# One-hot loads on another queue, an identity made on VectorE, two clears on GpSimd, and the mask tile's row copy issued earlier, in a fused block-sparse attention and low-rank mixer kernel

## The chip, the cores and the metric

The kernel runs on one core of a Trainium2 chip. The core has five engines that run side by side: TensorE (PE in the profile) for matrix products, with its weight load shown apart as PEld; VectorE (DVE); ScalarE (ACT); GpSimd (POOL); and SyncE (SP), which here only issues DMAs. The ending "q" (SPq, ACTq, POOLq) marks the sequencer of an engine, which issues DMAs and waits on semaphores. The metric is the device time of one execution in microseconds, lower is better.

## What is computed

Sparse attention over blocks of 32 tokens, then a mixer with a low-rank product along the sequence and a two-layer network. The reference, cut to what matters:

```python
B, H, S, D = 4, 8, 768, 64                 # q, k, v: float32
mask = window | first and last block row and column | 3 sampled blocks per row
scores = where(mask, q @ k.T / sqrt(D), -1e9)
attn   = softmax(scores) @ v
x = attn.transpose(0, 2, 1, 3).reshape(B, S, H * D)
u = x + (x.T @ U @ V).T                    # U: 768x32, V: 32x768
out = u + relu(u @ w_ch1) @ w_ch2          # w_ch1: 512x2048, w_ch2: 2048x512
```

## The kernel before

**Tiling.** The 4 x 8 heads are taken as 16 pairs of heads of one batch. Tokens lie as 128 partitions by T = 6. For each pair, q and k are loaded (`qld`, `kld`, L153, or L182 for the first pair), cast to fp16 (`stqld`, `stkld`), turned so that the head dimension lies on partitions, and then, for each block of 128 keys, TensorE makes scores transposed (keys on partitions, all 768 queries along the row), ScalarE takes exp into `est` (L996 for one block, L1014 for two), and TensorE multiplies `est` with `vt` (L421), whose 65th column of ones gives the sum. VectorE divides (L551, L558).

**Two ways to mask.** For the first four pairs (batch 0) the mask is added inside the score product: the operands `qres` and `kres` (parts of the tile `res`) hold 64 rows of q or k and 24 more rows. In `qres` the 24 rows are a one-hot code of the query's block (`one_hot_const`, 24 x 768); in `kres` they are the mask bias of each key column. There are two such sets, `qres[0]`/`kres[0]` for pairs 0 and 2 and `qres[1]`/`kres[1]` for pairs 1 and 3. Within a set the two heads of the pair use the rows 64 to 87 and 0 to 23 (`mrows`), the unused rows being zero. For the later pairs a 0/1 tile `mask` is multiplied after exp (L1052). `mask` is made in twelve pieces by products of the tile `kmask` (24 bias rows, the rest zero) with `qres[0]` (`mask_part`, L946, evaluated by VectorE at L952).

**The start.** The body of the kernel up to line 349 is written out by hand: each engine runs its instructions in exactly the order in which they are written (`manual_schedule`). It loads q and k of the first pair, one head at a time (`first_load`), the constants `small` (block mask, indices and an fp16 identity) and the sampled blocks `sb` (L245, L246, ScalarE's queue). TensorE runs idle products (`keep_warm`, L272) until the data is there. The first head is turned straight from fp32 with an fp32 identity `id32` (L226); the result is copied into `qres[0]` and `kres[0]` by ScalarE and VectorE (`first_row`, L297). Meanwhile VectorE makes the bias from `sb` (L311, L315, L318); the product of bias and one-hot rows (`mask_half`, L279) gives the 24 mask rows, which `mask_row` (L287) copies into `kres[0]`. The second head of the first pair is cast by GpSimd (L213), turned from fp16 (`last_turn`, L359) and copied (L366).

**After the start** a long string `PLAN` gives the order of everything else: each word is one step (S and B scores, e their exp, A value products, R the turning of the next pair's q or k, K one `mask_part`, and so on). The engines follow it in order.

**Queues.** SP issues nearly all loads, one after the other: an issue that has to wait holds up all that is written behind it. The order on SP at the start is: q and k of head 0; the two one-hot loads of `qres[0]` (L187); q and k of head 1; v of pair 0; q, k and v of pair 1; U (L200); then `second_set` (L192 to L196): one-hot rows and a copy of the mask rows for each head of set 1, and last the copy of the mask rows to `kmask`; then V (L206) and the loads of pair 2. The loads on SP and ScalarE report on eight completion semaphores, used in turn in program order, so that the ninth load waits until the first one has landed, and so on: v of pair 0 waits for `small`, q of pair 1 for the first head's q, k of pair 1 for `sb`, v of pair 1 for the first head's k, U for the first one-hot load. In the same way the copy to `kmask` waits for q of pair 1, V for k of pair 1, and q of pair 2 for v of pair 1.

From pair 5 on, q and k are turned by DMA transposes (L395) into `qpl` and `kpl`; the score products are then L1037 and exp L1046. L692 and L767 are the two layers of the network, which fill TensorE from about 45 us to the end.

Of the kernel before, what the change touches and what calls it, by code (L numbers as in the profile page):

```python
# [12 lines left out]
FP32 = mybir.dt.float32  # L13
# [10 lines left out]
def kernel(  # L24
# [14 lines left out]
    nc = tc.nc  # L39
# [34 lines left out]
    ohT_dr = nc.inline_tensor(ohT_np, name="one_hot_const")  # L74
# [14 lines left out]
    def bank(n, shape, dtype):  # L89
        ap = PS[:, n, :]  # L90
        if dtype != FP32:
            ap = ap.bitcast(dtype)
        ap = ap[:, 0 : int(np.prod(shape[1:]))]
        return ap.rearrange("p (a b) -> p a b", a=shape[1]) if len(shape) > 2 else ap
# [3 lines left out]
    def psc2():  # L98
        ring["psc"] += 1
        return PS[:, (0, 3)[ring["psc"] % 2] :][:, 0:2]  # L100
# [4 lines left out]
    id16 = small[:, NB + 1 :].bitcast(FP16)  # L105
# [5 lines left out]
    kmask = consts.tile([P, S], FP16, name="kmask")  # L111
    res = consts.tile([P, 4, 2, S], FP16, name="res")
    qres = [res[:, i] for i in range(2)]
    kres = [res[:, 2 + i] for i in range(2)]
    drows = [slice(0, D), slice(D, P)]
    mrows = [slice(D, D + NB), slice(0, NB)]
# [5 lines left out]
    Ut = wpool.tile([P, T, P], FP16)  # L122
    Vt = wpool.tile([P, T, P], FP16)
# [36 lines left out]
    def load_v(i):  # L160
        b, hp = divmod(i, HP)
        if i >= DIRECT:
            load_cast(i, v, vts[b % 2][:, 2 * hp : 2 * hp + 2, :, 0:D])
            return
        ld = ldpool.tile([P, 2, T, D], FP32, tag="ldv", name="vld")
        nc.sync.dma_start(
            out=ld,
            in_=v[b, 2 * hp : 2 * hp + 2].rearrange("h (p t) d -> p h t d", t=T),
        )
        cast(vts[b % 2][:, 2 * hp : 2 * hp + 2, :, 0:D], ld)  # L170
# [5 lines left out]
    def first_load(h, n, queue):  # L176

        src, nm = ((q, "qld"), (k, "kld"))[n]
        if h == 0:
            lds[nm] = ldpool.tile([P, 2, T, D], FP32, tag="ld" + nm, name=nm)  # L180
            sts[0, nm] = stpool.tile([P, T, 2, D], FP16, tag="st" + nm, name="st" + nm)
        queue.dma_start(  # L182
            out=lds[nm][:, h], in_=src[0, h].rearrange("(p t) d -> p t d", t=T)
        )

    def one_hot(i, h):
        nc.sync.dma_start(out=qres[i][mrows[h], h, :], in_=ohT_dr.ap())  # L187

    warm = nc.const_aps.tensor(1.0, [P, 512], mybir.dt.bfloat16)
    bias = consts.tile([P, 2, D], FP16)  # L190

    def second_set():  # L192
        for h in range(2):
            one_hot(1, h)
            nc.sync.dma_start(out=kres[1][mrows[h], h, :], in_=kres[0][mrows[h], h, :])
        nc.sync.dma_start(out=kmask[mrows[0], :], in_=kres[0][mrows[0], 0, :])  # L196

    def load_mix_u():
        uld = ldpool.tile([P, T, R], FP32, tag="ldu", name="uld", bufs=1)
# [11 lines left out]
    def first_cast(h, n, copy):  # L211
        nm = ("qld", "kld")[n]
        copy(out=sts[0, nm][:, :, h], in_=lds[nm][:, h])  # L213
# [3 lines left out]
    id32 = consts.tile([P, P], FP32)  # L217

    def first_turn(n, c):

        nm = ("qld", "kld")[n]
        twos = ((0, 1, 2), ()) if n == 0 else ((0,), (1, 2))
        pt = pw[:, 1, 0:HS] if n == 0 else bank(5 + c, [P, HS], FP32)
        first_out[n, c] = pt
        for j, t in enumerate(twos[c]):
            nc.tensor.matmul(  # L226
                pt[:, j * P : (j + 1) * P],
                lds[nm][:, 0, 2 * t : 2 * t + 2].rearrange("p t d -> p (t d)"),
                id32,
                is_transpose=True,  # L230
                start=(j == 0), stop=(j == len(twos[c]) - 1), skip_group_check=True,
            )

    with tc.manual_schedule(
        engines={
            mybir.EngineType.PE,
            mybir.EngineType.DVE,
            mybir.EngineType.Activation,
            mybir.EngineType.SP,
            mybir.EngineType.Pool,  # L240
        }
    ):
        first_load(0, 0, nc.sync)
        first_load(0, 1, nc.sync)
        nc.scalar.dma_start(out=small, in_=small_dr.ap())  # L245
        nc.scalar.dma_start(  # L246
            out=sb[0:NB].rearrange("k z r w -> k (z r w)"),
            in_=sampled_blocks.bitcast(I32)
            .rearrange("z r -> (z r)")[None, :]
            .broadcast_to([NB, NB * 6]),  # L250
        )
        for h in (1, 0):
            nc.vector.memset(qres[0][(slice(D, P), slice(0, D))[h], h, :], 0.0)
            one_hot(0, h)
        nc.vector.memset(bias, 0.0)
        for h in range(2):
            nc.vector.memset(kres[0][(slice(D, P), slice(0, D))[h], h, :], 0.0)
        for n in range(2):
            first_load(1, n, nc.sync)
        for tile_ in (qres[1], kres[1]):  # L260
            nc.gpsimd.memset(tile_.bitcast(FP32), 0.0)
        for vt in vts:
            nc.gpsimd.memset(vt[:, :, :, D : D + 1], 1.0)
        first = consts.tile([P, 1], FP32)
        nc.scalar.activation(
            out=first, in_=nc.const_aps.tensor(1.0, [P, 1], FP32), func=AF.Exp
        )
        pw = psc2()

        def keep_warm(n, cols=512):  # L270
            for _ in range(n):
                nc.tensor.matmul(  # L272
                    pw[:, 0, 0:cols], warm[:, 0:P], warm[:, 0:cols], start=True, stop=True
                )

        pks = [bank(2, [P, HS], FP32), bank(7, [P, HS], FP32)]

        def mask_half(c):
            nc.tensor.matmul(  # L279
                pks[c],  # L280
                bias[0:NB].rearrange("k a z -> k (a z)"),
                qres[0][mrows[1], 1, c * HS : (c + 1) * HS],
                start=True, stop=True,
            )

        def mask_row(h, c, copy, lo=0, hi=HS):
            copy(  # L287
                out=kres[0][mrows[h], h, c * HS + lo : c * HS + hi],
                in_=pks[c][mrows[h], lo:hi],
            )  # L290

        def first_row(n, c, u, copy):
            t0, m = (0, 3) if n == 0 else ((0, 1), (1, 2))[c]
            dst = (qres, kres)[n][0][drows[0], 0, :].rearrange(
                "p (t u c) -> p t u c", u=2, c=P
            )
            copy(  # L297
                out=dst[:, t0 : t0 + m, u],
                in_=first_out[n, c][drows[u], 0 : m * P].rearrange(
                    "p (t c) -> p t c", c=P  # L300
                ),
            )

        neq = consts.tile([P, NB, 3], FP32)
        a01 = consts.tile([P, NB], FP32)
        nc.vector.memset(Ut, 0.0)
        nc.scalar.copy(out=id32, in_=id16)
        psc2()
        keep_warm(6)
        keep_warm(1, 256)  # L310
        nc.vector.tensor_tensor(  # L311
            out=neq[0:NB], in0=sb[0:NB, :, :, 0],
            in1=iota[:, :, None].broadcast_to([NB, NB, 3]), op=ALU.not_equal,
        )
        nc.vector.tensor_reduce(  # L315
            out=a01[0:NB], in_=neq[0:NB], axis=mybir.AxisListType.X, op=ALU.min
        )
        nc.vector.scalar_tensor_tensor(  # L318
            out=bias[0:NB, :, 0:NB], in0=a01[0:NB, None].broadcast_to([NB, 2, NB]),
            scalar=MASK_BIAS, in1=ms[:, None].broadcast_to([NB, 2, NB]),  # L320
            op0=ALU.mult, op1=ALU.max,
        )
        first_turn(0, 0)
        first_row(0, 0, 0, nc.scalar.copy)
        first_row(0, 0, 1, nc.scalar.copy)
        first_turn(1, 0)
        first_row(1, 0, 0, nc.vector.tensor_copy)
        mask_half(0)
        mask_row(0, 0, nc.vector.tensor_copy, 0, P)
        first_turn(1, 1)  # L330
        first_row(1, 0, 1, nc.vector.tensor_copy)
        mask_half(1)
        first_row(1, 1, 0, nc.scalar.copy)
        mask_row(0, 0, nc.vector.tensor_copy, P, HS)
        first_row(1, 1, 1, nc.vector.tensor_copy)
        mask_row(0, 1, nc.vector.tensor_copy)
        mask_row(1, 0, nc.vector.tensor_copy)
        mask_row(1, 1, nc.vector.tensor_copy)

        for n in range(2):  # L340
            first_cast(1, n, nc.gpsimd.tensor_copy)
        for tile_ in (Vt, kmask):
            nc.gpsimd.memset(tile_.bitcast(FP32), 0.0)
        load_v(0)
        load_qk(1)
        load_v(1)
        load_mix_u()
        second_set()
        load_mix_v()

# [840 lines left out]
```

## Time and profile before

| what | us |
|---|---|
| time before, median of 3 runs | 270.37 (269.97 to 270.89) |
| the profiled execution's own time | 270.59 |
| its span in the profile | 268.8 |
| TensorE busy | 262.3 (98%) |
| VectorE busy | 232.5 (86%) |
| ScalarE busy | 202.8 (75%) |
| GpSimd busy | 72.6 (27%) |

The span runs from the first to the last instruction that the profile shows; 1.8 us of the profiled execution's time lie around it. "Idle before" is the time in which an engine had nothing running ahead of an instruction, and the arrow names what ended it. A busy share of 98% says only that TensorE had some product in flight nearly always; the stages differ in what they wait for. The granted TensorE clock is full (1.00) in every stretch. Times of day below are microseconds from the start of the span.

### The profile page before, as it was taken

The page shows a single profiled execution, that of the slowest core. Times are in us where ns is not written, and L with a number is a line of the kernel's source. Part 1 is how long each engine was busy: PE and PEld are TensorE (multiplying, and loading weights), DVE is VectorE, ACT ScalarE, POOL GpSimd, SP SyncE. Part 2 cuts the span into 40 slices and gives each one's busy share as a digit, 9 for nine tenths or more (in the row PEclk, how much of TensorE's full clock was granted, in tenths as well). Part 3 has the DMA queues.
Part 4 walks back from the last instruction along what each step waited for, and adds up shares of the span by engine and source line. Part 5 has one row for each costly group of instructions (what it writes and reads, how often), then busy time and mean ns, then how long its engine had stood idle before and what let it go on. Part 6 is the DMA issues. An engine that isn't in the chain of part 4 may idle for free.

```text
span 268.8 us, 7294 instructions
## 1 busy us (share of the span) xinstructions
PE 262.3 (98%) x2999; PEld 182.1 (68%) x2999; DVE 232.5 (86%) x477; ACT 202.8 (75%) x265; POOL 72.6 (27%) x98
## 2 busy tenths in 40 slices
PE   8899999999999999999999999999999999999995
PEld 3577776565667778665666887565667788666884
DVE  6589988988999998867588997688998999999993
ACT  5989998897989666788898857788997944789200
POOL 4558307199072470070706160000000000000000
PEclk9999999999999999999999999999999999999999
DMA  6787998999999999998928998620200115400024
GB/s 184 243 277 263 212 195 177 189 132 173 135 159 118 123 81 99 287 103 90 91 34 76 97 99 154 219 39 7 56 0 2 39 44 117 159 2 0 2 98 137
DMA packets 88720, 31.66 MB, mean 118 GB/s; under 512 B 77104, under 2 KB 85840, under 8 KB 88688
## 3 DMA queue, kind: packets, MB, share of 16 engines
q0 software_dynamic: 49728, 10.10, 46.7%
q1 hardware_dynamic: 38492, 20.86, 32.6%
q8 instruction: 23, 0.38, 0.6%
q10 hardware_dynamic: 468, 0.26, 0.4%
q14 instruction: 9, 0.07, 0.1%
HBM read 27.67 MB, written 6.29 MB: 126 GB/s over the span
## 4 chain that ended last, share of the span: by engine, by line
PE 78%; DMA 9%; DVE 6%; ACT 3%; SPq 1%; issue 1%; POOL 0%; DVEq 0%; ACTq 0%
PE ps L767 32%; PE ps L692 22%; PE ps L421 10%; PE ps L1037 9%; DMA kpl<-stkld 3%; DMA vld<-in_v_dram 3%; DMA qld<-in_q_dram 2%; PE ps L987 1%; DMA kmask<-res 1%; ACT est L1046 1%; PE ps L1006 1%; PE ps L672 1%; DVE est L1052 1%; DVE xf L558 1%; DVE res L976 1%
## 5 line engine op out<-in xcount | busy, mean ns | idle before, releaser
L1046 ACT ACTIVATE est<-ps 128x1536 f16<-128x1536 f32 x72 | 100.6, 1450 | 19.0 <-PE ps L1037 19.0
L692 PE MATMUL ps<-uT,w1t 128*128 128x384 f16 x384 | 70.3, 326 | 0.0
L1052 DVE TENSOR_TENSOR est<-est,mask 128x1440 f16<-128x1440 f16 x72 | 63.5, 902 | 0.7 <-ACT est L1046 0.2
L692 PEld LDWEIGHTS <-w1t 128*128 128x128 f16 x384 | 35.6, 97 | 26.6 <-issue 6.8
L421 PEld LDWEIGHTS <-est 128*128 128x128 f16 x1152 | 40.5, 97 | 6.8 <-issue 3.0
L421 PE MATMUL ps<-vt,est 128*128 128x65 f16 x1152 | 43.3, 193 | 0.1
L767 PEld LDWEIGHTS <-hid 128*128 128x128 f16 x358 | 34.0, 98 | 6.6 <-issue 1.6
L704 ACT ACTIVATE hid<-ps 128x384 f16<-128x384 f32 x63 | 29.7, 496 | 4.7 <-PE ps L692 4.3
L1037 PE MATMUL ps<-qpl,kpl 64*128 64x512 f16 (+1 forms) x288 | 31.7, 325 | 0.2 <-DMA kpl<-stkld 0.2
L767 PE MATMUL ps<-w2t,hid 128*128 128x256 f16 x238 | 31.1, 273 | 0.0
L139 POOL DMA_DIRECT2D stqld<-in_q_dram x20 | 16.3, 820 | 54.2 <-DMA qpl<-stqld 53.9
L886 DVE TENSOR_TENSOR xf<-xf,ps 128x256 f32<-128x256 f32 x63 | 25.3, 414 | 4.1 <-PE ps L767 3.7
L706 DVE TENSOR_SCALAR hid<-ps 128x384 f16<-128x384 f32 x33 | 18.3, 554 | 8.8 <-PE ps L692 8.0
L767 PEld LDWEIGHTS <-sums 128*128 128x128 f16 x216 | 20.1, 98 | 4.4 <-issue 1.0
L996 ACT ACTIVATE est<-ps 128x768 f16<-128x768 f32 x30 | 22.5, 812 | 0.4 <-PE ps L987 0.3
L1037 PEld LDWEIGHTS <-kpl 64*128 64x128 f16 x288 | 12.3, 94 | 14.5 <-issue 9.1
L767 PE MATMUL ps<-res,sums 128*128 128x256 f16 x144 | 19.4, 273 | 0.0
L139 POOL DMA_DIRECT2D stkld<-in_k_dram x20 | 16.3, 819 | 8.9 <-DMA kpl<-stkld 8.0
L641 ACT CAST xh<-xf 128x384 f16<-128x384 f32 x24 | 11.0, 510 | 10.0 <-DVE xf L637 10.0
L558 DVE TENSOR_TENSOR xf<-ps,rcp 128x384 f32<-128x384 f32 x32 | 17.7, 553 | 0.8
L139 POOL DMA_DIRECT2D vt<-in_v_dram x20 | 16.3, 820 | 0.0
L767 PE MATMUL ps<-res,hid 128*128 128x256 f16 x120 | 15.9, 273 | 0.0
(119 smaller groups left out, 338.6 us busy)
## 6 DMA issues: line engine op xcount, KB each, us to landing
out_dram<-xf SPq DMA_DIRECT2D x18, 256.0 KB, 2.4
vld<-in_v_dram SPq DMA_DIRECT2D x6, 384.0 KB, 6.7
w1t<-in_moe_w_ch_dram POOLq DMA_DIRECT2D x4, 512.0 KB, 8.2
w2t<-in_moe_w_ch_dram POOLq DMA_DIRECT2D x4, 512.0 KB, 8.3
qld<-in_q_dram SPq DMA_DIRECT2D x5, 384.0 KB, 3.9
kld<-in_k_dram SPq DMA_DIRECT2D x5, 384.0 KB
stqld<-in_q_dram POOLq DMA_DIRECT2D x20, 96.0 KB, 3.7
stkld<-in_k_dram POOLq DMA_DIRECT2D x20, 96.0 KB, 4.3
```

Source lines behind the costliest of these rows:

```text
L139: nc.gpsimd.dma_start(out=dst[:, h], in_=src[b, 2 * hp + h].rearrange("(p t) d -> p t d", t=T),)
L421: nc.tensor.matmul(pav[:, sc, :], est[:, n, sc * P : (sc + 1) * P], vts[b % 2][:, 2 * hp + h, g, 0 : D + 1], start=(g == 0 and sc == 0), s ...
L558: nc.vector.tensor_tensor(out=dst, in0=pav[:, :, 0:D], in1=rcp[:, :, None].broadcast_to([P, T, D]), op=ALU.mult,)
L692: nc.tensor.matmul(pt, w1t[:, cc, jj * P : (jj + 1) * P], bts[b].uT[:, cc, c * HS : (c + 1) * HS], start=(cc == 0), stop=(cc == NCC - 1), ...
L704: nc.scalar.activation(out=dst, in_=pt, func=AF.Relu)
L706: nc.vector.tensor_scalar_max(out=dst, in0=pt, scalar1=0.0)
L767: nc.tensor.matmul(acc[key], lhsT, rhs, start=(first and i == 0), stop=(i == len(pairs_) - 1), skip_group_check=True,)
L886: nc.vector.tensor_add(out=x, in0=x, in1=acc[a, b, tau])
L996: lambda: nc.scalar.activation(out=dst, in_=ps, func=AF.Exp, scale=0.125),
L1037: nc.tensor.matmul(units[h][:, u * S + lo : u * S + hi], kT[drows[h], g * P : (g + 1) * P], qT[drows[h], lo:hi], start=True, stop=True, sk ...
L1046: nc.scalar.activation(out=both[h], in_=units[h].rearrange("p (g n) -> p g n", g=2), func=AF.Exp, scale=0.125,)
L1052: lambda: nc.vector.tensor_mul(out=masked(both[h]), in0=masked(both[h]), in1=masked(mask[:, 2 * j : 2 * j + 2, :]),),
```

## The change

```diff
-    def one_hot(i, h):
-        nc.sync.dma_start(out=qres[i][mrows[h], h, :], in_=ohT_dr.ap())
+    def one_hot(i, h, queue):
+        queue.dma_start(out=qres[i][mrows[h], h, :], in_=ohT_dr.ap())
...
     def second_set():
+        one_hot(1, 0, nc.sync)
+        nc.sync.dma_start(out=kmask[mrows[0], :], in_=kres[0][mrows[0], 0, :])
+        one_hot(1, 1, nc.sync)
         for h in range(2):
-            one_hot(1, h)
             nc.sync.dma_start(out=kres[1][mrows[h], h, :], in_=kres[0][mrows[h], h, :])
-        nc.sync.dma_start(out=kmask[mrows[0], :], in_=kres[0][mrows[0], 0, :])
...
         for h in (1, 0):
             nc.vector.memset(qres[0][(slice(D, P), slice(0, D))[h], h, :], 0.0)
-            one_hot(0, h)
+            one_hot(0, h, nc.scalar)
...
         for vt in vts:
             nc.gpsimd.memset(vt[:, :, :, D : D + 1], 1.0)
+        for tile_ in (Ut, kmask):
+            nc.gpsimd.memset(tile_.bitcast(FP32), 0.0)
...
-        nc.vector.memset(Ut, 0.0)
-        nc.scalar.copy(out=id32, in_=id16)
+        nc.vector.tensor_copy(out=id32, in_=id16)
...
-        for tile_ in (Vt, kmask):
-            nc.gpsimd.memset(tile_.bitcast(FP32), 0.0)
+        nc.gpsimd.memset(Vt.bitcast(FP32), 0.0)
```

Five things differ. The two one-hot loads of set 0 leave SP's queue, where they stood ahead of q and k of head 1, and go to ScalarE's queue behind `sb` and ahead of the load of the exp table (L265). The copy of the identity to fp32 goes from ScalarE to VectorE, to the place where VectorE cleared `Ut`. The clear of `Ut` goes to GpSimd, behind the ones of `vt`. The clear of `kmask` moves up on GpSimd from behind the second head's casts to the same place. On SP the copy to `kmask` moves from fifth to second place in `second_set`, and the two copies into `kres[1]` come last. The order of TensorE and the PLAN are the same.

The completion semaphores, given out in program order, shift with the moves: the copy to `kmask` now waits for k of the first pair's second head in place of q of pair 1; the second one-hot load of set 1 waits for the last one-hot load of set 0; the copies into `kres[1]` wait for v of pair 0 and for q of pair 1. The waits of the loads of pairs 0, 1 and 2 named above stay the same.

## The prediction

> **What bounds the kernel now.** I read the chain of waits first, then the timeline of the first 16 us, where every edit lies, then stretches of that part with their DMA share. In the chain (start, length, what):
>
> ```profile
> 3.85 6.40 DMA qld<-in_q_dram
> ...
> 10.31 3.85 DMA kmask<-res
> 14.17 0.05 issue
> 14.21 0.34 PE ps L946
> ...
> 36.50 7.01 DMA vld<-in_v_dram
> ...
> 44.51 8.23 DMA kpl<-stkld
> 52.75 0.05 issue
> 52.79 0.82 PE ps L1037 x8
> ```
>
> Up to 14.21 the chain is made of loads: SP's issues, then q of pair 1 landing at 10.25, then the copy to `kmask`, which could not be issued before that and lands at 14.16. From 14.21 TensorE leads, with one more stretch of transfers (34.7 to 52.8), and from 52.8 on it is TensorE nearly alone. The change touches only what comes before about 14.5. So the question is how much earlier TensorE and ScalarE stand there, and whether the later stretch keeps it. The timeline (start, length, engine, line; in brackets the idle time before and what ended it):
>
> ```profile
> 1.65 0.80 SPq L187 DMA_DIRECT2D res<-one_hot_const  x2
> 2.50 0.36 SPq L182 DMA_DIRECT2D qld<-in_q_dram  x1
> 3.26 0.28 ACT L307 CAST id<-small 128x128 f32<-128x128 f16 x1
> 4.53 1.42 ACT L297 CAST res<-ps 64x384 f16<-64x384 f32 x3 [0.99 <-PE ps L226]
> 4.86 0.32 PE L279 MATMUL ps<-res,bias 24*128 24x384 f16 x1 [0.16 <-DMA res<-one_hot_const]
> 5.81 0.50 POOL L213 CAST stqld<-qld 128x384 f16<-128x384 f32 x1 [3.21 <-DMA qld<-in_q_dram]
> 12.61 0.51 PE L960 MATMUL ps<-small,stkld 128*128 128x128 f16 x6 [0.41 <-POOL stkld L131]
> 13.99 1.45 ACT L1014 ACTIVATE est<-ps 128x1536 f16<-128x1536 f32 x1 [0.93 <-PE ps L1006]
> 14.21 0.10 PEld L946 LDWEIGHTS <-kmask 128*128 128x128 f16 x1 [0.20 <-DMA kmask<-res]
> ```
>
> Two short waits at the start (one-hot rows 0.16; the identity, for which the first turn's weight load idled 0.58 until 3.54), then exps without a gap, then the largest hole: TensorE cannot turn k of pair 1 before GpSimd has cast it at 12.55, which waited for its load at 11.67, and ScalarE idles 0.93 for the scores behind it. Last, 0.20 for `kmask`. The stretches (last two columns: DMA share, GB/s):
>
> ```profile
> 3.30:4.30 1.00, 1.00 (x6) 0.71 (x4) 0.69 (x4) 0.24 (x2) 0.00 (x0) 1.00 0.57 131
> 4.30:5.80 1.50, 1.34 (x7) 0.45 (x7) 0.84 (x4) 1.17 (x3) 0.00 (x0) 1.00 0.90 301
> ...
> 11.70:13.00 1.30, 0.89 (x16) 0.70 (x15) 1.11 (x2) 1.30 (x2) 0.83 (x1) 1.00 0.54 135
> 13.00:14.20 1.20, 1.13 (x19) 0.75 (x15) 0.96 (x2) 0.27 (x2) 1.12 (x2) 1.00 0.28 61
> ```
>
> From 3.3 to 4.3 the engines carry the two one-hot loads and little else (131 GB/s), before and after that 256 to 301 GB/s: a dent in the stream of loads, which otherwise runs in the order of issue.
>
> **The one-hot loads leave SP's queue.** Their two issues with gaps take SP from 1.65 to 2.50, so q and k of head 1 are issued 0.85 earlier. V of pair 0 next waits for `small`, which had landed by 3.26 (ScalarE used it then): it goes out between 2.53 and 3.26 instead of 3.38. The following three wait for q of head 0 (in use at 3.59), `sb` (in use at 3.60) and k of head 0 (in use by 4.29): issued between 0.12 and 0.85 earlier, still ahead of their data, because the stream is some 2 us behind the issues. How far does the stream move? Lower bound: only the idle share of the dent is won, 0.43 x 1.0 = 0.43 us. Upper bound: the full 0.85. The 72 KB of one-hot rows still have to be carried; at 301 GB/s that is 0.24, so 0.85 - 0.24 = 0.61, which I take. So q, k, v of pairs 0 and 1 land 0.6 earlier, k of pair 1 is cast by 11.94, and TensorE, whose earlier work leaves it free at 12.20 (12.61 - 0.41), or 12.0 with the start 0.2 earlier (below), turns it near 12.0: 0.61 won there (up to 0.9 if the stream gains more, since the 0.32 that TensorE waits for q of pair 1 at 11.18 would go too). ScalarE's exp moves from 13.99 to 13.38, and 0.3 of its 0.93 stays.
>
> The Trainium skill speaks against a larger gain here: "Trainium Kernel Development and Optimization", Key Constraints, says that DMAs of all issuing queues run on the same 16 engines and interleave, and that another issuing engine saves issue time alone. By that the dent would give its idle share only, 0.43, and the whole sum would be 0.63 instead of 0.81. The row 3.30:4.30 has both parts, idle engines and engines busy at less than half the rate, so the trace leaves open which holds.
>
> **The same loads on ScalarE's queue.** They wait for the two clears of VectorE (done by 1.77), so not at all behind `sb` (issued by 1.82). Each issue costs between 0.31 (SP's rows for the same load) and 0.69 (`sb` on this queue); I take 0.37, that of `small` on it. The exp table (1.28) then loads from 2.6 to 3.9 instead of 1.85 to 3.13, and its first exp (0.20) ends at 4.1; ScalarE is wanted at 4.53, so it is hidden. At 0.69 it would be 4.7: the first scores 0.2 late. Landing: on SP's queue, behind two big loads, the rows were there at 4.83. `sb` on ScalarE's queue landed 1.73 after its issue (1.82 to 3.55), which gives 2.2 + 1.7 = 3.9. With the 0.16 gone and some 0.05 from the identity, scores start about 0.2 earlier.
>
> **The identity on VectorE.** No row shows this copy there; bounds 0.11 (VectorE's smallest clear) to 0.56 (its 128x384 casts), I take 0.28, that of ScalarE's copy and of VectorE's 128x128 cast at L583. VectorE loses the 0.38 clear of `Ut` and idled 0.24 before L311 waited for `sb`: 0.62 of room, so L311 stays at 3.60; at 0.56 and a late `small` it would slip by 0.2. The identity is ready between 3.2 and 3.54 instead of 3.54, but the warm-up products occupy TensorE until about 3.5: gain 0 to 0.1.
>
> **The clears on GpSimd.** Two of 0.42 at 2.6 to 3.4, in an idle stretch of 3.21 that ends at 5.81 (5.2 when the loads land earlier): nothing. Without that cover they would delay the second head's cast by 0.84. The clear that leaves 7.08 frees time in which GpSimd waits 0.96 for v anyway.
>
> **The mask rows' copy.** It no longer waits for q of pair 1 (10.25), but for VectorE's mask rows (about 7.3). It still queues behind v of pair 1, whose landing at 13.0 lets SP go on with pair 2 (the issue at 13.07), and behind U and one small load, no longer behind three more. Between 13.0 and 14.2 the stream is thin (share 0.28), so each of those small ones matters: gain between 0 and 14.16 - 13.0 = 1.16, besides the 0.61. Only 0.20 is needed to take its wait away, which I count. Behind it now: the second one-hot load and both copies into `kres[1]`. The first copy is wanted by the products of pair 1 at 15.27; even if it were last to land, as `kmask` was at 14.16, 1.1 us are left. The second waits for q of pair 1 and holds back V and pair 2's loads, but these wait for k and v of pair 1 themselves, which land later. No cost.
>
> **Sum.** 0.61 (stream) + 0.20 (`kmask`) = 0.81 at 14.2; the 0.2 of the start is not added, since k's landing decides behind it. Behind 14.2 nothing is changed. Loads of pair 2 follow v of pair 1, so the transfers up to 52.8 (DMA share 0.9 and more from 14.2 on) start 0.6 earlier too, and the turn of pair 5 that ends at 52.75 comes as much earlier as TensorE does. The profiled execution took 270.59 (span 268.8 and 1.8 around it), which gives 269.8; it lay 0.22 above the median of 270.37, so the forecast is 270.37 - 0.81 = 269.56, say 269.6.
>
> **Rivals.**
> *More than the sum.* At 52.8 TensorE waits 0.17 for the DMA turn of pair 5 and ScalarE 1.13 for the scores behind it. That turn takes 8.23 because weight loads and loads share the engines. If the moved stream clears these loads before the turn, up to 0.7 of the 1.13 comes on top: 268.9. For it: v of pair 5 took 7.01 and the turn 8.23, against 2.4 for a store in the page's list of transfers. Against it: every transfer moves by the same 0.6.
> *Hidden.* TensorE's chain from 14.2 to 20 alternates with exps; if the dent gives nothing because the engines are merely kept busy by the one-hot rows wherever they are, only the 0.16 and 0.20 remain, both beside the 0.93: 270.3. Against it: the idle 0.43 is in the row.
> *Slower.* The one-hot rows share the engines with four big loads and land late; the place is the first mask product (L279), the price the delay of the first exp (6.28) less the 0.93 that ScalarE idles later. It decides from a landing 0.93 after 4.83, at 5.8; landed at 6.7 it costs 0.9: 271.3. For it: on SP's queue the first of them took 2.7 from the end of its issue (1.78 and 0.31 in the chain) to 4.83, the longest of the small loads. Against it: `sb`, 1.73 at the same DMA load. The Trainium skill, "DMA: Bandwidth & Descriptors", Queues, rings and completion order, has each engine go round between queues packet by packet; by that the rows do not wait out the big loads, and the landing stays near 4.
> *It does not do what it says.* The issue order of each engine follows the text, so little is left for this: 270.4.
>
> **Chances.** Forecast 0.55, more 0.20, hidden 0.07, slower 0.17, no effect 0.01. About 0.3% (0.81 us) is what a measurement of this kernel can tell from no change, and the sum lies on that bound: half of the forecast's 0.55 falls on either side. Faster: 0.27 + 0.20 = 0.47; within: 0.28 + 0.07 + 0.01 = 0.36; slower 0.17. The forecast's own range is 269.1 to 270.0 (0.43 alone, and 0.85 with the 0.20 and the start's 0.2). For 8 in 10 it reaches down over most of the larger case, 268.7, and up to where the slower case begins, 271.2.
>
> **What would show it.** Right: q of head 1 issued at 1.65; L226 by 3.55; L279 without a wait for one-hot rows; stretch 3.3 to 4.3 near 300 GB/s; k of pair 1 cast by 12.0; ScalarE's idle before 13.4 near 0.3; L946 without a wait for `kmask`, near 13.4; L1037 behind the DMA turn near 52.1. Wrong: ScalarE's table load after 4.5; a first exp after 6.3; k of pair 1 landing as before; a new wait of L1006 near 14.6 for copies into `res`; a turn at 52.8 as before, which would mean that the DMA stretch does not keep the gain.

## The result and the profile after

| what | before | after |
|---|---|---|
| median of 16 runs each, us | 270.56 (269.66 to 271.82) | 271.68 (270.24 to 273.05) |
| ratio after to before | | 1.0041, interval 1.0021 to 1.0061 |
| the profiled execution's own time, us | 270.59 | 272.23 |
| its span, us | 268.8 | 270.5 |
| start of the first exp, us | 6.28 | 7.84 |
| start of the sixth exp over two blocks (L1014, now L1015), us | 21.15 | 23.00 |

The changed kernel is slower by 0.41%, where I had forecast 0.81 us less. Line numbers shift by one to three with the edits: after, the turns are L227, the mask products L282, the score products L988 and L1007, their exps L997 and L1015.

The first 8 us hold the cause. The chain of waits of the kernel after (start, length, what):

```profile
1.13 0.69 ACTq L247
...
1.86 3.62 DMA res<-one_hot_const
...
5.53 0.47 PE ps L282
...
7.05 2.03 PE ps L988 x6
...
19.01 0.33 PE ps L988 x2
```

The chain no longer goes through SP's issues and the loads of q. It goes through `sb`'s issue on ScalarE's queue, then through the two one-hot loads, issued from 1.86, the first of which landed at 5.49, and from there on TensorE. Two things are to be seen. The rows that TensorE needs first landed 1.6 later than the 3.9 of the prediction. And the six score products of L988 take 2.03, 0.34 each, while two of the same shape later in the same chain take 0.33, 0.165 each: TensorE works at half its rate. The timeline of the kernel after (start, length, engine, line; in brackets the idle time before and what ended it):

```profile
1.66 0.43 SPq L182 DMA_DIRECT2D qld<-in_q_dram  x1
1.86 0.72 ACTq L187 DMA_DIRECT2D res<-one_hot_const  x2
2.61 1.28 ACT L268 ACT_TABLE_LOAD   x1 [2.61 <-DVE res L254]
3.06 0.30 DVE L309 CAST id<-small 128x128 f32<-128x128 f16 x1
3.50 0.85 PE L227 MATMUL ps<-id,qld 128*128 128x128 f32 x3
5.53 0.47 PE L282 MATMUL ps<-res,bias 24*128 24x384 f16 x1 [0.97 <-DMA res<-one_hot_const]
6.98 2.10 PE L988 MATMUL ps<-res 128*128 128x384 f16 x6
7.84 2.21 ACT L997 ACTIVATE est<-ps 128x768 f16<-128x768 f32 x3 [0.81 <-PE ps L988]
10.80 0.85 PE L360 MATMUL ps<-small,stkld 128*128 128x128 f16 x6
14.12 0.50 PE L961 MATMUL ps<-small,stkld 128*128 128x128 f16 x6
```

and the counterparts of two of these in the timeline of the kernel before:

```profile
5.74 1.40 PE L987 MATMUL ps<-res 128*128 128x384 f16 x6
6.28 2.21 ACT L996 ACTIVATE est<-ps 128x768 f16<-128x768 f32 x3 [0.33 <-PE ps L987]
```

What was moved off the path is off it: the loads of head 1 are issued at 1.66, the table load is over at 3.89, the identity is ready at 3.36. But TensorE waits 0.97 for the rows, and the first exp idles 0.81 for scores where it idled 0.33. Six turns of one shape, 0.85 at 10.80 and 0.50 at 14.12, show that the slow rate lasts beyond 10.8; the products are at full rate from 12.2 on. Before, the slow rate is gone when the first scores start.

The page's clock row says nothing of this (page of the kernel after, the line of the granted clock):

```profile
PEclk9999999999999999999999999999999999999999
```

It is full in every slice, those of the slow products too. The clock records in the trace, from which this row is made, do show the rate: the first one, at full clock, begins at 12.21 in the kernel after and at 4.56 in the kernel before, and the page counts the time ahead of it as full. The products agree: in the kernel after, those of 128 columns follow each other every 0.107 before 12.21 and every 0.056 behind it. So the clock that was read as full in every stretch of the kernel before was half up to 4.56. The rate has to be read from the start of the first record, or from the length of groups with one shape. The Trainium skill, "TensorE: Matmul & The Clock Gate", Part 1, describes such a rate: the array runs at half its clock until it has been busy for one activity window of about 3.4 us, and the window runs free, so that the moment varies from run to run. The factor of two and the variation agree with the traces here (0.34 against 0.165, and the moments in the table below). So does the window: in the 13 traces that have clock records the full clock lasts 259.41, 262.83 or 266.24, which is 76, 77 or 78 times 3.413.

The stretches in which the rows travel, of the kernel after (last two columns: DMA share, GB/s):

```profile
3.30:4.30 1.00, 1.00 (x6) 0.72 (x4) 0.69 (x4) 0.80 (x2) 0.00 (x0) 1.00 0.96 188
4.30:5.80 1.50, 0.53 (x3) 0.10 (x1) 0.28 (x1) 0.95 (x2) 0.00 (x0) 1.00 0.78 228
```

The dent that the rows made on SP's queue (share 0.57, 131 GB/s) is filled, 0.96 and 188 GB/s. The price is in the rows themselves. In the traces' packet records their 48 packets start from about 3.35 to 4.00 before, a block between the big loads; after, they are strewn from 3.38 to 5.46 among the loads of head 1. Both times they begin when q and k of head 0 (384 KB on SP's queue) have passed, at about 3.35: the rows started no sooner on the other queue, and took 2.1 instead of 0.65.

### The profile page after: what moved, and what is told of

The parts are those of the page before. It is cut to its first block, busy times and chain, and to the rows that moved or that the text cites. A ratio compares the mean times of both kernels' runs of the same rounds, so it can differ in the third digit from the quotient of the medians.

```text
span 270.5 us, 7292 instructions
## 1 busy us (share of the span) xinstructions
PE 264.3 (98%) x2999; PEld 183.6 (68%) x2999; DVE 232.6 (86%) x477; ACT 202.7 (75%) x264; POOL 72.9 (27%) x99
## 3 DMA queue, kind: packets, MB, share of 16 engines
q1 hardware_dynamic: 38420, 20.79, 33.4%
## 4 chain that ended last, share of the span: by engine, by line
PE 83%; DMA 7%; DVE 5%; ACT 2%; issue 1%; ACTq 0%; POOL 0%; DVEq 0%; POOLq 0%
PE ps L768 32%; PE ps L693 21%; PE ps L422 10%; PE ps L1038 9%; DMA qpl<-stqld 4%; PE ps L988 4%; PE ps L1007 3%; DMA stqld<-in_q_dram 2%; ACT est L1015 2%; DMA res<-one_hot_const 1%; PE ps L673 1%; DVE est L1053 1%; PE ps L947 1%; DVE xf L559 1%; PE ps L961 0%
## 5 line engine op out<-in xcount | busy, mean ns | idle before, releaser
L997 ACT ACTIVATE est<-ps 128x768 f16<-128x768 f32 x30 | 22.5, 812 | 1.4 <-PE ps L988 1.4
```

Of the source, the lines that this page charges most:

```text
L997: lambda: nc.scalar.activation(out=dst, in_=ps, func=AF.Exp, scale=0.125),
```

## What was tried

The table has, for the profile of each kernel that ran, the start of the first mask product (M), the idle time of TensorE just before it, which the rows cause if nothing else is said, the stretch from M to the first exp, the stretch from that exp to the sixth one over two blocks, when it starts, and the execution's own time. "Fast from" is the start of the first clock record; e8 has none, and its 4.0 is read from the distances of the products.

| kernel | M | idle before M | M to exp | exp to sixth | sixth | fast from | time |
|---|---|---|---|---|---|---|---|
| before | 4.86 | 0.16 | 1.42 | 14.87 | 21.15 | 4.56 | 270.59 |
| f2_before_again | 4.90 | 0.39 | 1.43 | 14.33 | 20.66 | 3.70 | 270.50 |
| after | 5.53 | 0.97 | 2.31 | 15.16 | 23.00 | 12.21 | 272.23 |
| f1_after_again | 5.08 | 0.52 | 2.31 | 14.29 | 21.68 | 9.08 | 270.83 |
| e1_fill | 5.67 | filled | 1.44 | 14.14 | 21.25 | 5.05 | 270.37 |
| e2_rows_on_sp | 4.81 | 0.13 | 2.31 | 14.64 | 21.76 | 9.52 | 271.16 |
| e3_rows_alone | 5.57 | 0.11, see text | 2.31 | 14.95 | 22.83 | 11.82 | 272.37 |
| e4_cold | 5.06 | 0.34, a copy of VectorE | 2.30 | 14.40 | 21.76 | 9.29 | 270.90 |
| e5_decoy | 4.95 | 0.38 | 2.31 | 14.49 | 21.75 | 9.37 | 271.14 |
| e6_kmask_alone | 4.78 | 0.08 | 1.60 | 14.11 | 20.49 | 5.29 | 269.93 |
| e7_sp_fill | 5.23 | filled | 1.42 | 14.14 | 20.79 | 5.00 | 269.93 |
| e8_split_fill | 5.05 | 0.36 | 1.42 | 14.14 | 20.61 | 4.0 | 269.94 |
| e9_before_fill | 4.75 | filled | 1.44 | 14.59 | 20.78 | 4.37 | 269.89 |
| f3_sp_fill2 | 5.06 | filled | 1.42 | 14.18 | 20.66 | 3.73 | 269.83 |

In all 14 profiles the span is the start of the sixth two-block exp plus 247.3 to 248.1, so a delay at 21 us reaches the end nearly whole. The stretch from M to the first exp has two values, 1.42 to 1.44 and 2.30 to 2.31 (with one between, where the first of the two mask products is slow and the rest fast).

**Fill the wait (e1_fill).** The changed kernel, with four more unused warm-up products in TensorE's order where it waits for the rows.

```diff
+        keep_warm(4)
         mask_half(0)
```

> The changed kernel with four more warm-up products (128x512) ahead of the first mask product, where TensorE waited 0.97 us for the one-hot rows. Theory A (the late rows let TensorE's clock fall, and six microseconds of products at half rate cost more than the wait itself): products stay at full rate behind 5.5 (the six score products some 1.4 us as before the change, not 2.1), the rows still land near 5.5, the first exp comes at 6.9 to 7.1 instead of 7.84, and the time is 270.2 to 270.7, some 1.0 to 1.4 below the changed kernel. Rival B (the late landing itself costs, through the order of transfers): the products at full rate change little, 271.3 to 271.8.

Median 270.72 (12 runs), ratio to before 1.0001 (0.9979 to 1.0023). Timeline of this kernel:

```profile
5.67 0.33 PE L282 MATMUL ps<-res,bias 24*128 24x384 f16 x1
6.57 1.40 PE L989 MATMUL ps<-res 128*128 128x384 f16 x6
7.11 2.21 ACT L998 ACTIVATE est<-ps 128x768 f16<-128x768 f32 x3 [0.33 <-PE ps L989]
```

The mask product is 0.14 later than in the kernel after, and the kernel is faster all the same, since the first scores take 1.40 instead of 2.10. Time and first exp lie just above what was expected. So the idle time counts for the rate first and for the delay second. The delay alone behaves nearly as the prediction's rival had it: the first exp is 0.83 later than before, the sixth two-block exp 0.10.

**The rows back on SP's queue (e2_rows_on_sp).** The changed kernel with the old queue for set 0; the rest of the change stays.

```diff
-            one_hot(0, h, nc.scalar)
+            one_hot(0, h, nc.sync)
```

> The changed kernel with the two one-hot loads of set 0 back in their old place on SP's queue; identity, clears and mask copy stay changed. Theory A: rows land near 4.8, no cold stretch, no loss; the remaining edits give 0 to 0.4, so 270.0 to 270.5. Rival C (the reordered mask copy or the clears cost): still 271 or more.

Median 270.85, ratio 1.0005 (0.9983 to 1.0026): the loss is gone, though the time lies above what was expected. The profile surprised me (timeline):

```profile
4.81 0.47 PE L282 MATMUL ps<-res,bias 24*128 24x384 f16 x1
6.27 2.10 PE L988 MATMUL ps<-res 128*128 128x384 f16 x6
```

Hardly a wait for the rows (0.13), and yet the slow rate, until 9.5. Its twelve times fall into two groups, five of 269.41 to 270.02 and seven of 270.71 to 271.48, about the worth of the rate. A wait for the rows is thus not the only thing that keeps the rate low; executions of one kernel differ.

**The rows alone (e3_rows_alone).** The kernel before with nothing changed but the queue of these two loads.

```diff
-    def one_hot(i, h):
-        nc.sync.dma_start(out=qres[i][mrows[h], h, :], in_=ohT_dr.ap())
+    def one_hot(i, h, queue=nc.sync):
+        queue.dma_start(out=qres[i][mrows[h], h, :], in_=ohT_dr.ap())
...
-            one_hot(0, h)
+            one_hot(0, h, nc.scalar)
```

> The kernel before with nothing changed but the queue of the two one-hot loads of set 0 (ScalarE's instead of SP's). Theory A: all of the loss is here, 271.4 to 272.2, with rows landing near 5.5 and products at half rate behind it; the identity, still on ScalarE behind these issues and the table load, adds up to 0.6 us at the first turn. Rival C: 270.4 to 270.8.

Median 272.07, ratio 1.0050 (1.0031 to 1.0069). The whole loss is in this one edit. Here the identity is late too, because ScalarE still makes it, behind the later table load: the first turn waits 0.64 for it and starts at 4.35, the mask product at 5.57. The rows landed at 5.53, so TensorE lost only 0.11 more to them. VectorE's identity takes the first wait away in the full change, but TensorE only waits longer for the rows instead.

**The rate alone (e4_cold).** The kernel before with fewer warm-up products at the start; no load is moved.

```diff
-        keep_warm(6)
+        keep_warm(2)
```

> The kernel before with two warm-up products of 512 columns instead of six, all else equal: a gap of some 1.5 us ahead of the first turn, no transfer moved. Theory A (clock alone): the score products run at half rate for some microseconds though the rows land at 4.8; 0.6 to 1.5 us slower, 271.0 to 272.0. Rival B: the same time as before within 0.3.

Median 271.27, ratio 1.0041 (1.0021 to 1.0062). Timeline of this kernel:

```profile
3.60 0.90 PE L226 MATMUL ps<-id,qld 128*128 128x128 f32 x3 [1.60 <-ACT id L307]
6.50 2.10 PE L987 MATMUL ps<-res 128*128 128x384 f16 x6
```

The first turn starts at the same 3.6 as before, after an idle stretch of 1.60, and the scores run slow until 9.3. By the ratio that alone costs as much as the whole change; by the medians, 271.27 against 270.73 of the kernel before on the same chip, about half. The mask product is 0.20 later here, so not quite all of it is the rate.

**Why the rows are late (e5_decoy).** The changed kernel with two extra loads of the same rows on SP's queue in the old place, into a tile that is idle at that time, so that the loads of head 1 are issued late again; one profiled execution.

```diff
         for h in (1, 0):
+            nc.sync.dma_start(out=hid[mrows[h], h, 0:2].rearrange("p j n -> p (j n)"), in_=ohT_dr.ap())
             one_hot(0, h, nc.scalar)
```

> The changed kernel with two more loads of the same one-hot rows into an idle tile, on SP's queue in the old place; they hold the loads of head 1 back (these also wait for the constants, so they are issued behind 3.0 instead of at 1.66). The rows that count still go over ScalarE's queue. Theory D (they are late because head 1's loads share the engines with them): they land at 4.3 to 4.9, and the wait of 0.97 at the first mask product is 0 to 0.3. Rival E (ScalarE's queue itself is late): they land near 5.5 and the wait stays near 0.9.

```profile
4.95 0.47 PE L283 MATMUL ps<-res,bias 24*128 24x384 f16 x1 [0.38 <-DMA res<-one_hot_const]
```

That is the first mask product in this kernel's timeline. The rows land at 4.91, just later than expected, and their packets start from 3.28 to 4.37. One landing says little, since the unaltered changed kernel had one at 5.04 (below). The packets say more: they are spread over 1.1 here and over 1.9 to 2.1 in the four profiles (after, f1, e1, e3) in which the rows went over ScalarE's queue with the loads of head 1 early. ScalarE's queue is therefore not slow by itself; what stretched the rows was mostly the loads of head 1, which the change had moved up beside them.

**Full rate with the rows on SP's queue (e7_sp_fill, f3_sp_fill2), with one row set on each queue (e8_split_fill), and before with a fill (e9_before_fill).** e7 and e9 add one warm-up product of 512 columns ahead of `mask_half(0)`, to e2 and to the kernel before; f3 adds two to e2; e8 is e7 with the load for h = 0 on ScalarE's queue, as `one_hot(0, h, (nc.scalar, nc.sync)[h])`.

```diff
+        keep_warm(1, 512)
         mask_half(0)
```

> The changed kernel with the one-hot loads of set 0 back on SP's queue and one more warm-up product (128x512) ahead of the first mask product. Theory A (what is left of the loss with the rows on SP is the clock, which rose in some executions and not in others): products at full rate from 5.7 on in nearly every execution, 269.6 to 270.2, 0.2 to 0.4% faster than before. Rival C: as with the rows on SP alone, 270.5 to 271.0.

> As the kernel with the rows on SP and one more warm-up product, but only the one-hot load that the first mask product needs (second head's rows) is on SP; the other one is on ScalarE's queue. Theory A with D: the first lands near 4.8, the other by 5.7, head 1's loads are issued 0.4 earlier than before, the start is not delayed: 269.4 to 270.0. Rival: the second load, late on ScalarE's queue, holds the first score product (weights of L988) beyond 6.3: 270.5 or more.

> The kernel before with one more warm-up product (128x512) ahead of the first mask product, nothing else. Theory A: the kernel before also starts with the clock low in part of its executions, so its slower ones go: 269.9 to 270.4, 0.1 to 0.3% faster in the median. Rival: the product only delays the first mask product by 0.2 to 0.4, 270.7 to 271.1.

> The changed kernel with the one-hot rows on SP and two more warm-up products (128x512) ahead of the first mask product instead of one. If the clock rises more surely, no execution is over 271.5 and the median is 269.8 to 270.2. If the filling only shifts the moment, some executions stay over 271.5 and the median is 270.2 to 270.8, since the second product delays the first mask product by 0.2 to 0.4.

Ratios to before: e7 0.9991 (0.9967 to 1.0016), e8 1.0032 (0.9999 to 1.0065), e9 1.0013 (0.9988 to 1.0038), f3 0.9990 (0.9972 to 1.0008). All four profiles show the full rate by 5.0 and the first exp at 6.19 to 6.65; in e8, e9 and f3 it was there (4.0, 4.37, 3.73) before the added product, so of these four only e7 bears on what filling does for the rate. None is told from before by its median. f3 came out as expected for a clock that rises more surely, with the narrowest spread, 269.39 to 270.51, against 269.59 to 271.43 of the kernel before on the same chip. e7 still has two of its twelve runs over 271.8. e8 is inconclusive: its profiled execution took 269.94, yet half of its runs are over 271.5, and no profile caught one of those. e9 shows what then holds the kernel before: its TensorE waits 0.53 for `kmask` at 13.9.

**The mask rows' copy alone (e6_kmask_alone).** The kernel before with the copy to `kmask` in second place and the clear of `kmask` moved up.

```diff
         for vt in vts:
             nc.gpsimd.memset(vt[:, :, :, D : D + 1], 1.0)
+        nc.gpsimd.memset(kmask.bitcast(FP32), 0.0)
...
-        for tile_ in (Vt, kmask):
-            nc.gpsimd.memset(tile_.bitcast(FP32), 0.0)
+        nc.gpsimd.memset(Vt.bitcast(FP32), 0.0)
...
+        one_hot(1, 0)
+        nc.sync.dma_start(out=kmask[mrows[0], :], in_=kres[0][mrows[0], 0, :])
+        one_hot(1, 1)
         for h in range(2):
-            one_hot(1, h)
             nc.sync.dma_start(out=kres[1][mrows[h], h, :], in_=kres[0][mrows[h], h, :])
-        nc.sync.dma_start(out=kmask[mrows[0], :], in_=kres[0][mrows[0], 0, :])
```

> The kernel before with the copy to the mask tile moved to second place, its clear moved up on GpSimd, nothing else. The prediction's term: the wait of TensorE for the mask tile is gone and the time falls by up to 0.2, more (up to 0.5) in executions that start with the clock high, where this wait was 1.2 us in the kernel before with one more warm-up product: 270.2 to 270.7. Rival C (the copies into the second operand set, now last, or the shifted completion semaphores hold something back): 271.0 or more.

Median 270.12, ratio 1.0004 (0.9986 to 1.0022). In the profile the wait for `kmask` is gone and the sixth exp starts 0.2 to 0.7 sooner than in the two profiles of before, but the median shows no gain.

**Both kernels once more (f1_after_again, f2_before_again).** One profiled execution of each, unchanged.

> The changed kernel once more, unaltered, for its profile. Its times spread from 270.2 to 273.1. Theory A (the spread is the moment at which TensorE's clock rises, which differs from one execution to the next): if this execution takes under 271, its score products are at full rate (0.32 apart or less) before 7.5; if it takes over 271.8, they are at half rate to 11 or 12. Rival: the rate of the first products is as in the first profile (half until 11.7) whatever the time. In both the rows land at 5.3 to 5.7.

> The kernel before once more, unaltered, for its profile. Theory A: the same rule; under 270.6 full rate from 5 on, over 270.9 half rate to 9 or later; the rows land at 4.7 to 4.9 in either. Rival: full rate from 5 on whatever the time.

The changed kernel's second profile (timeline):

```profile
5.08 0.47 PE L282 MATMUL ps<-res,bias 24*128 24x384 f16 x1 [0.52 <-DMA res<-one_hot_const]
6.53 2.10 PE L988 MATMUL ps<-res 128*128 128x384 f16 x6
9.40 0.50 PE L360 MATMUL ps<-small,stqld 128*128 128x128 f16 x6
```

Again a wait for the rows, shorter, and again slow scores; but the full rate comes at 9.1 instead of 12.2, not before 7.5 as the expectation had it for a time under 271. The execution is 1.4 faster than the first. In the kernel before the second profile shows the full rate at 3.7, which both the theory and the rival had expected, a wait of 0.39 for the rows that comes too late to matter for it, and a cast of k of pair 1 that starts at 11.10 instead of 11.72 with nothing changed.

## Why the prediction was wrong

**The ledger.** With e1 as the mark for what the changed kernel does at full rate, the 1.85 by which the sixth two-block exp is later in the profiles comes apart:

| term | working | us |
|---|---|---|
| M starts later | 5.53 - 4.86 | +0.67 |
| slow rate, M to first exp | 2.31 - 1.42 | +0.89 |
| slow rate, first exp to the sixth | 15.16 - 14.14 (e1) | +1.02 |
| what the change wins behind the first exp | 14.87 - 14.14 | -0.73 |
| sum | 23.00 - 21.15 | +1.85 |

The span grows by 1.6 (268.81 to 270.45). The median grows by 1.12, since executions differ in when the full rate comes: the second profile has 0.22, 0.89, 0.15 and the same -0.73, in all 0.53.

**The step that failed** is "Landing" in the part on the same loads on ScalarE's queue. The prediction took `sb`'s 1.73 and put the rows at 3.9; they landed at 5.49, and at 5.04 in the second profile. By the 2.7 that its rival "Slower" had from the rows themselves it would have been 2.2 + 2.7 = 4.9. `sb`'s packets had begun at 2.64, beside q and k of head 0 alone; those of the rows began at 3.38, with head 1's loads already issued: the part on the stream moved these up by 0.85 and did not ask what they would meet on the engines. The Trainium skill's rule of rounds between queues, which the prediction cited against a late landing ("DMA: Bandwidth & Descriptors", Queues, rings and completion order), agrees with the strewn packets, but not with the conclusion drawn from it: to be interleaved with big loads cost more (2.1 for the rows) than to stand between them in one queue (0.65).

**The missing term** is TensorE's rate. No step of the prediction priced it, although the trace before shows the warm-up products whose work it is. The rival "Slower" had the place right, the first mask product, and the late landing. But the landing measured, 5.49, lies ahead of its point of decision, 5.8, so by its own price, the delay less 0.93, nothing would have been lost. For the delay alone that is about what e1 shows (0.83 late, 0.73 given back). The 0.89 and 1.02 of the rate are what decided, and e4 shows that they need no late load at all.

**The stream, 0.61.** The mechanism came: head 1's loads were issued 0.85 earlier, the dent was filled, k of pair 1 was cast at 10.58 instead of 11.72. Its worth did not. First, in the profile after, TensorE now stood 1.5 us behind and turned that k only at 14.12. Second, the hole that the 0.61 was to close belonged in the main to one execution: f2 casts k at 11.10 and e6, whose loads of head 1 stand where they stood before, at 10.68, and in neither does TensorE wait for it (0.23 in e9, 0.41 in before). e6 reaches 14.11 from the first exp to the sixth without the moved loads, as good as e1 with them. So I sized a term by a wait that varies from execution to execution by as much as the term.

**The copy to `kmask`, 0.20.** Right in kind: the wait is gone in after, e1, e6 and e7. In before it is 0.20, 0.3 to 0.4 in f2 and 0.53 to 0.65 in e9, so it grows where the wait for k is short or absent. Its worth lies below what the medians tell.

**Hidden edits.** The table load (2.61 to 3.89, forecast 2.6 to 3.9), its first exp (over at 4.11, forecast 4.1), the identity (0.30 on VectorE, 0.28 taken) and the clears on GpSimd (over at 3.28, forecast 3.4) came as forecast and cost nothing. The stretch at 52.8 does not bind in the profile after the change, where TensorE arrives at 54.40. With TensorE there sooner it varies: TensorE waits 0.17 to 0.63 for the DMA turn in before, f2, e2 and e6, and not at all in e1, e7, e9 and f3, which are there at 52.06 to 52.64.

**What stays open.** What decides the moment of full rate in a single execution is settled in part. TensorE's first product starts at 0.77 or 0.78 in all 14 profiles. Counted back from the rise in steps of 3.413, the first window that ends later than 3.6 ends at another time in each: at 5.29 in e6, 5.38 in after, 5.67 in f1, 6.10 in e2. The rise comes at that end, or one or two windows later. The Trainium skill, "TensorE: Matmul & The Clock Gate", Part 1, says that the windows run free of the kernel's start; the traces agree. e6 and after have this end at nearly the same place: with hardly a wait the rate rises there, with a wait of 0.97 only at 12.21. Where the wait is filled it rises there too (e1 5.05, e7 5.00), and where 0.64 is spent on the identity it does not (e3, 4.99, rises at 11.82). In f2 the window ends at 3.70, before the wait, which then does no harm. The window of e2 fails without such a wait, and how full a window has to be is not worked out here: TensorE is busy for 3.28 of the 3.41 in the one from 2.69 to 6.10 in e2, which fails, and for 2.92 in the one from 0.29 to 3.70 in f2, which does not. So a part of the rate's price in single profiles is the place of the windows and not the change; that the change loses in the median rests on the runs of after, e1 and e3. How often before starts fast is known from two profiles alone, which both did, and e8's slow half is unexplained. The rows on GpSimd's queue were not tried.

## What to carry to other kernels

A wait of TensorE in its first microseconds is priced by the rate that it puts off, not only by its length: in one execution here 0.97 us of waiting went with 1.9 us lost to slow products behind it. A small load that was needed first stood well ahead of the bulk in the same queue; moved to another queue, with the bulk moved up beside it, it came late. And a wait read from one profile is a term of a sum only after a second profile has shown it too.

## What was not expected of the hardware

- The full rate came at 3.7 to 5.3, at 9.1 to 9.5 or at 11.8 to 12.2, and it differed between executions of the same kernel (9.1 and 12.2) as between kernels; the page's row of the granted clock is full throughout, because the trace's first clock record begins only there.
- An idle stretch of 0.97 or 1.60 us within the first 6 us went with the later moments, and unused products ahead of the mask products with the earlier ones in all five kernels that had them (in e8, e9 and f3 the rate was full before them). The rows on SP's queue without such a product (e2) went with 9.5 although the wait there was 0.13. The Trainium skill, "TensorE: Matmul & The Clock Gate", Part 1, names idle times of about a window, 3.4 us, for the clock to fall; the runs here show far shorter gaps, 0.97 us, to matter while it has not yet risen.
- 72 KB in 48 packets took 0.65 between big loads of one queue and 2.1 beside them on another.
